# Two batches take turns in the sums of their shared chunk, and the planner's ranks are drawn anew

## The chip, the cores and the metric

The kernel runs on one core of a Trainium2 chip. The time is device microseconds (us) of one execution; lower is better. Several executions are timed and the median is told, and one more execution is profiled: it has a time of its own, and its span runs from its first instruction to its last.

## The reference

Attention with random features over 8 batches of 8 heads, 576 tokens and 64 channels, with 128 features, and behind it a bilinear feed-forward network over all 4608 tokens:

```
def phi(x):                                   # x scaled by 64 ** -0.25
    h = x @ omega.T - sum(x * x) / 2
    return exp(h - max(h)) / sqrt(128)
kv  = einsum('bhsm,bhsd->bhmd', phi(k), v)    # one 128 x 64 matrix per batch and head
z   = sum(phi(k), axis=2)
att = (phi(q) @ kv) / (phi(q) @ z + 1e-6)
x   = att, heads side by side                 # 4608 x 512
out = (((x @ w1) * (x @ w2)) @ w3) @ w_out    # 512 -> 1024 -> 1024 -> 512
```

## The kernel before

**Tiles.** The 4608 tokens are 36 chunks of 128 rows. A batch has 576 tokens, four chunks and a half, so chunk 4 belongs to batch 0 with its first 64 rows and to batch 1 with its last 64.

**Keys and values.** For each chunk TensorE projects the keys (`kpj`, L610 in float32 for the first chunks, L615 in pairs of float16 later), VectorE takes the maximum over the features (L643), ScalarE the exponential (L665), and the result is split into two float16 parts (L527 to L531, L686). The sum over the tokens of features times values, `kvp`, is made in float32 from whole features for batches 0 and 1 (L769, `kv_add`), and from the float16 parts for the six others (L822). `kv_add(b, n)` adds the share of batch `b` in its chunk `n`: for each of two groups of four heads one step of four matmuls, into the PSUM bank `kvp_b_g`. The whole chunks use all 128 rows of the array. The two shares of chunk 4 use rows 0 to 63 and rows 64 to 127; batch 0's two steps come first and close its banks, then batch 1's two steps open theirs. When the last share of a batch is in, ScalarE moves its two banks out (L782, `kv_exact`), and `kv_parts` makes float16 parts of them. The profile shows each float32 matmul as two records.

**Queries.** They go the same way, then are turned by DMA (`eqT`), multiplied by the batch's matrix (`nu`, L902 and L908), divided and turned again (`xT`).

**Weights.** They arrive as 64-bit floats, 1 MB at a time (L1054, into one of three places called `raw`), and ScalarE, VectorE and GpSimd make float32 of them in five steps (L1057, L1063, L1066, L1070, L1079). The product of `w3` and `w_out` is made in eight blocks of sixteen float32 matmuls (`wp`, L1150). `w1` and `w2` get sums of their magnitudes (`l`, L1106), a scale (`ws`, L1123) and float16 parts (L1133).

**The network.** For chunks 0 to 7 it is `gate` (`ab`, L1196), from chunk 8 on `seven_gate`, a form with seven block products in place of eight (`x` and `y`, L1303); `project_out` multiplies by the product matrix (`o`, L1530).

**The order.** No loop fixes it. Each step is an operation with an assumed duration, and the class `Plan` replays all of them: an engine that is free takes, of the operations whose inputs and buffers are there, the one with the lowest rank. The order that comes out is written into the program. A rank is a place in a hand-made timetable (`KRANK`, `QRANK`, `WRANK`, and a period of 15.1 for the later chunks) plus a correction from the table `SHIFT`, by kind and number. Loads carry `hold`: they are not begun before their rank, read as a time. Buffers of most kinds are given out in turn. Where TensorE would have nothing to do before 260 us of the replay, the plan puts in a matmul on constants, the filler (`warm`, L459). It needs a free PSUM bank of the kind `pm`, of which there are four; the sums `kvp` of batches 0 and 1, the blocks `wp`, `ab`, `x`, `y`, `o` and the small sums of squares use the same four.

Of the kernel before, what the change touches and what calls it, by code (L numbers as in the profile page):

```python
# [22 lines left out]
P = 128  # L23
# [30 lines left out]
class Plan:  # L54
# [211 lines left out]
KV_PARTS = 4.7  # L266
# [3 lines left out]
    "attend": [-261.0442, -899.7197, -80.5697, -1.7498, -497.6982, -829.27, -0.5233, 130.4034, -60.6807, -977.3105, 590.9, -139.0417, -1108.6767, -258.3056, 152.0799, -675.3894, 179.9762, -129.9433, -156.7907, -531.4993, -603.8193, 184.7717, 169.6617, -1403.3389, 90.1091, -577.3232, 242.8103, 80.48, 87.4543, -540.7832, -24.3105, 130.0178, 497.3243, -219.6722, -908.4751, -817.6591],  # L270
    "fetch": [-320.1924, -257.6749, -303.305, -248.9927, -252.9728, -161.6177, -170.7265, -141.0951, 0.0, -68.9231, 11.8978, 0.0, 18.3653, -56.175, -98.2639, -172.3054, -4.3852, 8.0229, 6.9409, 11.3851, 0.0, 9.4996, 8.3504],
    "gate": [45.0201, -55.6099, 53.21, -242.9426, 211.0326, -147.4938, -186.7604, -112.2666, 234.1896, -62.4668, 351.9161, -553.5163, -101.3645, -184.3984, 21.6502, -6.2693, 205.244, 884.0132, 0.0, 0.0, -146.1711, -55.9723, 0.0, 0.0, 105.9104, 213.7739, 0.0, 0.0, 74.0634, 182.5986, 0.0, 0.0, -59.026, 392.9282, 0.0, 0.0, -269.9867, 15.1283, 0.0, 0.0, -416.4902, -203.1226, 0.0, 0.0, -26.4861, 683.023, 0.0, 0.0, 107.705, 121.6833, 0.0, 0.0, 369.2073, 337.3498, 0.0, 0.0, 253.0506, 236.1074, 0.0, 0.0, -273.608, -60.1419, 0.0, 0.0, -120.9892, -52.692, 0.0, 0.0, 12.4493, -100.2414],
# [20 lines left out]
EXACT_B = 2  # L293
# [40 lines left out]
def tile_favor_attention_then_bilinear_ffn(  # L334
# [383 lines left out]
    def v_batch(b):  # L718
# [18 lines left out]
        for c, r0, r1 in cs:  # L737
# [3 lines left out]
            def ends(t=t, r0=r0, r1=r1):  # L741
                if r1 - r0 < P:
# [11 lines left out]
                    t.ap[r0:r1, 0, :, 0:D], ALU.mult, ALU.subtract,  # L754
                ),
                r=[x, s, (t, 0)], w=[(t, 1)], port=BOTH)

    kv_sum = [[Buf("pm", f"kvp_{b}_{g}") for g in range(2)] for b in range(EXACT_B)]

    def kv_add(b, n):  # L760
        cs = chunks_of(b)
        c, r0, r1 = cs[n]
        last = n == len(cs) - 1

        def add(g):
            t = kv_sum[b][g].ap[:, 0 : 4 * E].rearrange("p (i e) -> p i e", e=E)
# [821 lines left out]
    for c in range(NCH):  # L1588
# [26 lines left out]
        if c >= PROJECT_K and c - AHEAD >= alone:  # L1615
            plan.at("q", c - AHEAD, q_rank(c - AHEAD))
            q_chunk(c - AHEAD, c - AHEAD < FAST_Q)
# [95 lines left out]
```

## Time and profile before

| | |
|---|---|
| median of 3 timed runs | 776.56 us (773.46 to 778.33) |
| the profiled execution: its time, its span | 771.27 us, 769.5 us |
| TensorE busy | 746.3 us (97%), 10458 instructions |
| VectorE busy | 639.0 us (83%) |
| ScalarE busy | 488.7 us (64%) |
| GpSimd busy | 263.7 us (34%) |
| mean granted clock of TensorE | 0.999 |
| read from and written to HBM | 49.50 MB and 9.44 MB |

Engines are named PE (TensorE matmuls), PEld (its weight loads), DVE (VectorE), ACT (ScalarE), POOL (GpSimd) and SP (SyncE, which issues DMAs). A granted clock of 1.00 is the higher of TensorE's two levels, 2.4 GHz. Busy time counts fillers too.

### The profile page before, as it was taken

Reading aid. Unit: us, or ns where it says so; the run is one execution under the profiler, and the core shown is the slowest. Engines: PE = TensorE matmul, PEld = TensorE weight load, DVE = VectorE, ACT = ScalarE, POOL = GpSimd, SP = SyncE. Lnnn points to the kernel's source line nnn. Section 1 sums busy time; section 2 is a strip of 40 time slices with the busy share of each in tenths; the row PEclk is TensorE's granted clock in tenths of the full one; section 3 lists DMA queues with packets and bytes.
Section 4 is the critical chain, followed back from the end, with each engine's and each line's share of the span. In section 5 each row is a group of like instructions: output and inputs, shape, how many; then the busy total and the mean of one; then the engine's idle time right before and its main releaser. Section 6 shows DMA issues by size and latency. Waiting matters only on the chain.

```text
span 769.5 us, 24553 instructions
## 1 busy us (share of the span) xinstructions
PE 746.3 (97%) x10458; PEld 589.1 (77%) x10466; DVE 639.0 (83%) x1178; ACT 488.7 (64%) x952; POOL 263.7 (34%) x314
## 2 busy tenths in 40 slices
PE   8999999999999999999999999999999999999998
PEld 7756558886757787778787868789877968789784
DVE  6899899999998878979989899998798687787332
ACT  5857575787898956867776568675665455434221
POOL 2301005535621434254442275624433162511000
PEclk9999999999999999999999999999999999999999
DMA  9897852333463645555456447553543345444101
GB/s 340 308 260 219 233 152 84 112 98 72 103 145 112 143 114 86 118 85 148 105 95 146 112 112 174 104 112 78 105 98 77 84 84 116 79 97 72 42 15 42
DMA packets 166909, 93.82 MB, mean 122 GB/s; under 512 B 136976, under 2 KB 145296, under 8 KB 166800
## 3 DMA queue, kind: packets, MB, share of 16 engines
q1 hardware_dynamic: 158784, 79.60, 44.0%
q10 hardware_dynamic: 8016, 12.65, 5.2%
q8 instruction: 82, 1.34, 0.7%
q14 instruction: 27, 0.22, 0.1%
HBM read 49.50 MB, written 9.44 MB: 77 GB/s over the span
## 4 chain that ended last, share of the span: by engine, by line
PE 52%; DVE 29%; DMA 6%; ACT 5%; issue 5%; POOL 2%; SPq 0%; ACTq 0%; DVEq 0%; POOLq 0%
PE o L1530 14%; PE x L1303 13%; PE y L1303 10%; PE ab L1196 4%; PE wp L1150 3%; PE nu L908 2%; DVE nm_k L643 2%; PE qpj L615 2%; DVE arena L1070 2%; DVE nm_q L643 2%; PE kvp L822 2%; DMA arena<-wo 2%; DMA eqT<-eq 1%; DVE eq L686 1%; DVE vhl L752 1%
## 5 line engine op out<-in xcount | busy, mean ns | idle before, releaser
L1303 PEld LDWEIGHTS <-arena 128*128 128x128 f16 x2688 | 152.9, 98 | 6.1 <-issue 1.8
L1303 PEld LDWEIGHTS <-w12b 128*128 128x128 f16 x2016 | 114.3, 98 | 3.3
L1530 PE MATMUL o<-Wb,w12b 128*128 128x512 f16 x408 | 93.8, 379 | 0.0
L1196 PE MATMUL ab<-xT,w12b 128*128 128x128 f16 (+1 forms) x1152 | 88.7, 237 | 1.6 <-DVE ws L1123 1.3
L1196 PEld LDWEIGHTS <-w12b 128*128 128x128 f16 x1152 | 80.4, 98 | 10.3 <-issue 2.0
L1303 PE MATMUL x<-xT,arena 128*128 128x128 f16 x1344 | 84.2, 219 | 0.8 <-ACT u_u L1320 0.4
L1303 PE MATMUL y<-xT,arena 128*128 128x128 f16 x1344 | 84.2, 219 | 0.5 <-DVE asb_s L1326 0.5
L1303 PE MATMUL x<-xT,w12b 128*128 128x128 f16 x1344 | 82.5, 219 | 0.0
L1530 PEld LDWEIGHTS <-w12b 128*128 128x128 f16 x408 | 38.5, 98 | 42.4 <-issue 0.5
L1530 PE MATMUL o<-Wb 128*128 128x512 f16 x276 | 63.8, 379 | 0.2 <-POOL Wb L1337 0.2
L1530 PEld LDWEIGHTS <-Wb 128*128 128x128 f16 x276 | 26.0, 98 | 29.1 <-POOL Wb L1337 0.7
L643 DVE TENSOR_REDUCE nm_q<-qpj 128x8 f32<-128x1024 f32 x36 | 43.7, 1215 | 5.0 <-PE qpj L615 5.0
L643 DVE TENSOR_REDUCE nm_k<-kpj 128x8 f32<-128x1024 f32 x36 | 43.6, 1215 | 2.8 <-PE kpj L615 1.9
L1539 ACT ACTIVATE o<-o,oscs 128x512 f32<-128x512 f32 x36 | 24.8, 688 | 33.0 <-PE o L1530 30.0
L676 ACT ACTIVATE e_q<-e_q,ln_e,es_q 128x1024 f32<-128x1024 f32 x25 | 31.0, 1240 | 19.0 <-DVE e_q L672 14.1
L1530 PE MATMUL o<-Wb,arena 128*128 128x512 f16 x180 | 41.7, 379 | 0.5 <-ACT asb L1208 0.5
L1303 PE MATMUL y<-xT,w12b 128*128 128x128 f16 x672 | 42.1, 219 | 0.0
L686 DVE TENSOR_TENSOR eq<-e_q,eq 128x1024 f16<-128x1024 f32 x26 | 33.6, 1292 | 4.5 <-ACT eq L527 3.4
L1324 DVE TENSOR_TENSOR u_u<-x,u_u 128x512 f32<-128x512 f32 x28 | 19.2, 687 | 20.9 <-PE x L1303 20.4
L908 PEld LDWEIGHTS <-eqT 128*128 128x128 f16 (+1 forms) x936 | 29.4, 100 | 7.7 <-issue 3.1
L908 PE MATMUL nu<-kv,eqT 128*128 128x65 f16 (+1 forms) x936 | 32.0, 193 | 2.6 <-DMA eqT<-eq 2.3
L1000 ACT ACTIVATE xw_x<-xw_x,p2r_x 128x512 f32<-128x512 f32 x28 | 20.0, 717 | 21.7 <-DVE p2r_x L520 21.3
(238 smaller groups left out, 1633.3 us busy)
## 6 DMA issues: line engine op xcount, KB each, us to landing
vraw<-v SPq DMA_DIRECT2D x36, 260.0 KB, 3.7
qraw<-qT SPq DMA_DIRECT2D x36, 256.0 KB, 3.0
kraw<-kT SPq DMA_DIRECT2D x36, 256.0 KB, 3.2
out<-o SPq DMA_DIRECT2D x36, 256.0 KB, 2.4
arena<-w3T ACTq DMA_DIRECT2D x6, 1024.0 KB, 5.9
arena<-w ACTq DMA_DIRECT2D x6, 1024.0 KB, 5.3
arena<-wo SPq DMA_DIRECT2D x4, 1024.0 KB, 7.5
arena<-w3T SPq DMA_DIRECT2D x2, 1024.0 KB, 7.5
```

Source lines behind the costliest of these rows:

```text
L615: nc.tensor.matmul(pg[:, g, i], hls[name, c].ap[d, x, i], om[d, y], start=n == 0, stop=n == len(PASSES) - 1)
L643: one(DVE, 1.22, lambda: nc.vector.tensor_reduce(nm.ap, pj_of(pa), AX.X, ALU.max, negate=True), r=[pa], w=[nm], new=[nm])
L676: one(ACT, 1.23, lambda: nc.scalar.activation(e.ap, e.ap, AF.Exp, scale=factor(), bias=ln_e), r=key, w=[e])
L686: engine(g).tensor_tensor(f16(t.ap)[:, 1], e.ap, f16(t.ap)[:, 0], ALU.subtract)
L908: nc.tensor.matmul(n_[r0:r1, h // 4, h % 4], f16(t.ap)[:, x, place(h), r0:r1], kv_view(kvs[b])[:, y, h], start=n == 0, stop=n == 2,)
L1000: one(ACT, 0.72, lambda: nc.scalar.mul(flat(xs), flat(xs), r.ap), r=[r], w=[xs])
L1150: nc.tensor.matmul(bank.ap, w[:, j], guest[:, j], start=j == 0, stop=j == NF - 1)
L1196: nc.tensor.matmul(dst, w12[m][i][cc][:, a, r * P : (r + 1) * P], x.ap[:, b, cc, off : off + T], start=j == 0, stop=j == len(mm) - 1,)
L1303: nc.tensor.matmul(dst()[:, f * P : (f + 1) * P], ws[c][0]()[:, a, f * P : (f + 1) * P], xv(c, b), start=start and f == 0 and j == 0, stop ...
L1324: one(DVE, 0.69, lambda: nc.vector.tensor_tensor(f32(t), dst(), f32(t), ALU.add), r=[key], w=[t], rank=first)
L1530: nc.tensor.matmul(bank.ap, hs[c, f][1]()[:, a], W[f][:, b], start=f0 + i == 0, stop=f0 + 4 == NF and i == len(mm) - 1,)
L1539: one(ACT, 0.67, lambda: nc.scalar.mul(o.ap, bank.ap, sc), r=[bank, ("osc", c)], w=[o], new=[o], rank=rank - 1000)
```

## The change

`kv_add` takes a list of shares. A whole chunk has one share and is added as before. Chunk 4 has two, and they are one call now: for each group of four heads one step of eight matmuls, in which for each head batch 0's matmul on rows 0 to 63 is followed by batch 1's on rows 64 to 127, into their two banks. So the step holds a bank of each batch, and opens batch 1's while it closes batch 0's. The plan assumes 0.62 us for such a step, where it assumed 0.94 us for each of four smaller ones, and batch 1's extra delay of `KV_PARTS` is gone; the two shares have one rank, that of number 4 of the kind `kv`, and number 5 is not used. Besides, every number of `SHIFT` that was not zero is another one: all ranks of all kinds. Of the 22 kinds the diff shows three here.

```diff
-    "fetch": [-320.1924, -257.6749, -303.305, -248.9927, -252.9728, -161.6177, -170.7265, -141.0951, 0.0, -68.9231, 11.8978, 0.0, 18.3653, -56.175, -98.2639, -172.3054, -4.3852, 8.0229, 6.9409, 11.3851, 0.0, 9.4996, 8.3504],
+    "fetch": [-925.3345, -824.8687, -542.9285, -450.6918, -535.714, -378.1459, -382.3202, -197.542, 0.0, -64.6442, -36.7066, 0.0, -41.7227, -79.9913, -175.1455, -278.5055, -110.7568, -9.3466, -14.5852, -15.7422, 0.0, -0.7951, -23.1963],
...
-    "kv": [158.5124, -158.4609, -162.7804, -150.9707, -232.8124, -145.8852, -391.2947, -100.8073, 3.6608, -482.1456],
+    "kv": [-100.7299, -528.6885, -690.7509, -418.2748, 112.2776, 0.0, 423.4926, -147.2643, 569.9348, 218.7368],
...
-    "unit": [-522.9387, -317.9578, -322.7961, -303.0594, -300.9332, -217.673, -199.3355, -141.0736, -973.4887, -80.9006, 14.191, -73.1609, 23.3492, -24.603, -104.8843, -198.5929, -11.0785, 15.999, -2.7909, 29.5605, 81.4712, 34.6026, 111.1784, 182.8732, 238.4257],
+    "unit": [-1451.7847, -1375.0192, -1357.2705, -1064.5022, -1000.9318, -710.22, -563.0267, -429.5976, 266.1431, -5.4514, 14.5282, 104.5733, 38.5182, -52.7715, -121.3134, -488.4972, -94.1638, 6.3287, 168.2541, 222.0637, 349.3645, 304.6784, 412.186, -18.4507, 84.1356],
...
-    def kv_add(b, n):
-        cs = chunks_of(b)
-        c, r0, r1 = cs[n]
-        last = n == len(cs) - 1
+    def kv_add(*shares):
 
         def add(g):
-            t = kv_sum[b][g].ap[:, 0 : 4 * E].rearrange("p (i e) -> p i e", e=E)
             for i in range(4):
                 h = 4 * g + i
-                nc.tensor.matmul(
-                    t[:, i], ekf[c].ap[r0:r1, place(h)], vraw[c].ap[r0:r1, h],
-                    start=n == 0 and i == 0, stop=last and i == 3,
-                )
-
+                for b, n in shares:
+                    cs = chunks_of(b)
+                    c, r0, r1 = cs[n]
+                    t = kv_sum[b][g].ap[:, 0 : 4 * E].rearrange("p (i e) -> p i e", e=E)
+                    nc.tensor.matmul(
+                        t[:, i], ekf[c].ap[r0:r1, place(h)], vraw[c].ap[r0:r1, h],
+                        start=n == 0 and i == 0, stop=n == len(cs) - 1 and i == 3,
+                    )
+
+        c, r0, r1 = chunks_of(shares[0][0])[shares[0][1]]
         for g in range(2):
-            one(PE, 0.94, lambda g=g: add(g), r=[ekf[c], (vraw[c], 0), (vraw[c], 1)],
-                w=[kv_sum[b][g]], new=[kv_sum[b][g]] * (n == 0), mode=P if r1 - r0 == P else D)
+            banks = [kv_sum[b][g] for b, _ in shares]
+            one(PE, 0.94 if r1 - r0 == P else 0.62, lambda g=g: add(g), r=[ekf[c], (vraw[c], 0), (vraw[c], 1)],
+                w=banks, new=[kv_sum[b][g] for b, n in shares if n == 0], mode=P if r1 - r0 == P else D)
...
+        shares = [(b, n) for b in range(EXACT_B) for n, x in enumerate(chunks_of(b)) if x[0] == c]
+        if shares:
+            plan.at("kv", c + shares[0][0], r)
+            kv_add(*shares)
         for b in range(EXACT_B):
-            for n, (x, _, _) in enumerate(chunks_of(b)):
-                if x == c:
-                    plan.at("kv", c + b, r + (KV_PARTS if b and not n else 0))
-                    kv_add(b, n)
             if last_of.get(c) == b:
```

The numbers of `unit` and `fetch` follow the string `ooooWW11a22bWWWWWW11a22bS`: `o` is a quarter of `w_out`, `W` a block of the product, `1` and `2` a quarter of `w1` or `w2`, `a` and `b` the split of a half of `w1` or `w2`, `S` the split of the product.

## Rows read from the trace of the kernel before

**Rows 1.** The page, part 1, TensorE alone; part 2, its granted clock.

```profile
PE 746.3 (97%) x10458; PEld 589.1 (77%) x10466; DVE 639.0 (83%) x1178; ACT 488.7 (64%) x952; POOL 263.7 (34%) x314
...
PEclk9999999999999999999999999999999999999999
```

**Rows 2.** Busy time by stage; sixth column of engines is granted clock.

```profile
0.00:36.00 36.00, 32.84 (x314) 27.64 (x315) 28.87 (x42) 23.84 (x65) 9.51 (x34) 1.00 0.93 332
36.00:160.00 124.00, 117.74 (x1099) 82.55 (x1106) 115.21 (x197) 80.93 (x167) 29.36 (x28) 1.00 0.61 172
160.00:460.00 300.00, 291.00 (x4310) 230.60 (x4308) 266.81 (x516) 226.26 (x468) 125.41 (x142) 1.00 0.51 113
460.00:765.66 305.66, 304.71 (x4748) 248.31 (x4744) 228.16 (x425) 156.97 (x255) 99.44 (x111) 1.00 0.40 87
765.66:769.50 3.84, 0.00 (x1) 0.00 (x0) 0.00 (x0) 0.69 (x1) 0.00 (x0) 0.88 0.17 68
```

**Rows 3.** The same stages, instructions on the tile warm alone.

```profile
0.00:36.00 36.00, 9.79 (x66) 0.20 (x1) 1.00 0.93 332
36.00:160.00 124.00, 6.00 (x52) 0.00 (x0) 1.00 0.61 172
```

**Rows 4.** Waits of TensorE, 0 to 160 us: total, times, longest.

```profile
PE l L1106 <- ACT o_wab L1098: 1.7, 1, 1.7
PE wp L1150 <- DVE arena L1079: 1.5, 1, 1.5
PE ab L1196 <- DVE ws L1123: 1.3, 1, 1.3
PE wp L1150 <- DVE xT L1079: 1.3, 1, 1.3
```

**Rows 5.** The same list for 160 to 460 us.

```profile
PE norm_q L493 <- ACT junk L487: 3.4, 5, 1.2
PE nu L908 <- DMA eqT<-eq: 2.3, 2, 1.6
```

**Rows 6.** Timeline of TensorE, 0 to 60 us: start, length, what, idle before.

```profile
26.69 2.00 PE L769 MATMUL kvp<-vraw,ek_f 128*128 128x65 f32 x16
29.03 1.16 PE L610 MATMUL kpj<-o_om_raw,kraw 64*128 64x128 f32 x16 [0.34 <-ACT ek_f L665]
30.02 2.40 PE L769 MATMUL kvp<-vraw,ek_f 64*128 64x65 f32 x24
32.79 1.10 PE L769 MATMUL kvp<-vraw,ek_f 64*128 64x65 f32 x8 [0.37 <-ACT kv_f L782]
...
33.87 1.47 PE L459 MATMUL warm<-ones 128*128 128x256 bf16 x12
35.47 7.11 PE L1150 MATMUL wp<-w12b,xT 128*128 128x512 f32 x16
```

**Rows 7.** Timeline of all engines, 28 to 37 us.

```profile
31.32 1.14 ACT L1057 ACTIVATE arena<-arena 128x1024 f32<-128x1024 f32 x1 [2.35 <-DMA arena<-w3T]
...
32.35 0.66 ACT L782 ACTIVATE kv_f<-kvp 128x260 f32<-128x260 f32 x2
...
34.11 1.22 DVE L1079 SCALAR_TENSOR_TENSOR xT<-arena 128x1024 uint32<-128x1024 uint32 x1
```

**Rows 8.** Timeline of SyncE, 0 to 60 us: its DMA issues.

```profile
2.12 0.43 SPq L1054 DMA_DIRECT2D arena<-wo  x1
...
18.31 0.38 SPq L1054 DMA_DIRECT2D arena<-wo  x1
```

**Rows 9.** Busy time in the stretch 100 to 220 us.

```profile
100.00:220.00 120.00, 114.21 (x1479) 91.99 (x1483) 116.54 (x216) 91.09 (x198) 56.49 (x45) 1.00 0.40 102
```

**Rows 10.** Groups by line and shape: VectorE work of one key chunk.

```profile
L643 DVE TENSOR_REDUCE nm_k<-kpj 128x8 f32<-128x1024 f32 x36 | 43.6, 1215 | 2.8 <-PE kpj L615 1.9 <-PE kpj L610 0.7
...
L686 DVE TENSOR_TENSOR ek<-e_k,ek 128x1024 f16<-128x1024 f32 x17 | 21.6, 1270 | 1.5 <-ACT ek L527 0.9 <-POOL ek L531 0.4
...
L590 DVE SCALAR_TENSOR_TENSOR hlk_k<-kraw,s_q,hlk_k 128x512 f16<-128x512 f32 x25 | 20.6, 823 | 0.0
```

More of the change, by code (lines that the diff above doesn't have):

```diff
@@ L272 @@
-    "gate": [45.0201, -55.6099, 53.21, -242.9426, 211.0326, -147.4938, -186.7604, -112.2666, 234.1896, -62.4668, 351.9161, -553.5163, -101.3645, -184.3984, 21.6502, -6.2693, 205.244, 884.0132, 0.0, 0.0, -146.1711, -55.9723, 0.0, 0.0, 105.9104, 213.7739, 0.0, 0.0, 74.0634, 182.5986, 0.0, 0.0, -59.026, 392.9282, 0.0, 0.0, -269.9867, 15.1283, 0.0, 0.0, -416.4902, -203.1226, 0.0, 0.0, -26.4861, 683.023, 0.0, 0.0, 107.705, 121.6833, 0.0, 0.0, 369.2073, 337.3498, 0.0, 0.0, 253.0506, 236.1074, 0.0, 0.0, -273.608, -60.1419, 0.0, 0.0, -120.9892, -52.692, 0.0, 0.0, 12.4493, -100.2414],
[9 rows of a table removed]
@@ L282 @@
-    "out": [-376.514, 497.2412, 63.8815, -68.9294, -790.7933, 891.007, -0.2063, 162.7468, -307.3469, 677.8557, 275.8913, 105.9823, 300.0604, -563.3277, 370.8116, 1120.3123, -636.2116, 38.8286, -5.1696, 269.1214, 780.3382, 886.5999, 899.8989, -746.3036, 532.6139, 601.5237, -365.0474, -87.4787, 222.8698, -417.0185, -590.3117, -61.4904, -1288.133, 152.0269, 215.2352, -197.548],
-    "pair": [0.0, 0.0, 0.0, 0.0, 0.0, 0.0, 0.0, 0.0, 0.0, 0.0, 0.0, -69.1469, -420.1598, -350.3318, -1467.0095, 13.5062, -1262.8946, 161.0739, 3.1468, -107.8226, -868.2686, -207.1637, -4.9551, -125.6928, 59.6855, -846.6351, 70.1117, -179.4445, 39.5746, -99.3894, -178.0142, 666.0484, -383.5356, 215.1784, 582.7228, 3.0289],
[5 rows of a table removed]
@@ L289 @@
-    "sum": [11.8372, 1491.9104, -128.3876, 359.8411],
-    "unit": [-522.9387, -317.9578, -322.7961, -303.0594, -300.9332, -217.673, -199.3355, -141.0736, -973.4887, -80.9006, 14.191, -73.1609, 23.3492, -24.603, -104.8843, -198.5929, -11.0785, 15.999, -2.7909, 29.5605, 81.4712, 34.6026, 111.1784, 182.8732, 238.4257],
-    "v": [0.0, 0.0, 289.4843, -41.9162, 317.7933, 338.429, 193.7706, 295.9627],
+    "attend": [-33.9644, -588.7958, -245.2466, 112.6694, 51.3394, 623.7508, -211.7652, -49.8193, 1.1812, -586.9079, 1809.2974, -184.659, -2377.44, -259.9265, -49.4813, -2.2019, -105.5111, 198.3123, 28.0357, -56.1994, -123.9714, 5.3923, -19.9446, 86.3289, 70.3568, 186.7349, 77.7578, 454.5261, -23.0736, -693.9705, -159.068, -511.3347, -748.5079, -72.6846, 331.0986, 368.0839],
@@ new lines @@
+    "fetch": [-925.3345, -824.8687, -542.9285, -450.6918, -535.714, -378.1459, -382.3202, -197.542, 0.0, -64.6442, -36.7066, 0.0, -41.7227, -79.9913, -175.1455, -278.5055, -110.7568, -9.3466, -14.5852, -15.7422, 0.0, -0.7951, -23.1963],
+    "gate": [481.8676, 164.6381, 249.9083, 992.1741, 1575.3487, -332.7836, -306.4834, -286.4339, -368.3007, -330.7792, 89.3306, -106.6537, -152.6991, 63.7717, 469.0214, 553.3953, -28.276, 962.2678, 0.0, 0.0, -1724.903, -89.3212, 0.0, 0.0, -941.0957, -54.4385, 0.0, 0.0, -46.177, -47.5723, 0.0, 0.0, -184.5281, 130.4981, 0.0, 0.0, 161.2236, 270.4674, 0.0, 0.0, 409.8437, 393.5028, 0.0, 0.0, 133.38, 619.7029, 0.0, 0.0, 278.6571, 446.1498, 0.0, 0.0, 657.3535, -170.8092, 0.0, 0.0, -59.2993, 25.8461, 0.0, 0.0, 297.6619, 266.9017, 0.0, 0.0, -605.7172, 238.8639, 0.0, 0.0, 203.6933, 325.2007],
[9 rows of a table added]
@@ new lines @@
+    "out": [400.6419, 663.3448, 676.3232, 88.4737, 76.7119, 1035.9881, 1201.8732, 591.8491, -1466.2665, 351.619, -510.5236, 436.3716, 847.5083, 709.8632, 93.8906, 30.7097, -588.3518, 486.9493, 722.7325, -262.5307, 1540.2584, -47.0963, 641.4933, -854.8927, -421.9015, 1090.9892, 37.749, -55.6569, 103.9235, 946.5714, -411.2674, -596.0518, 264.3718, 519.464, 581.4619, -211.4359],
+    "pair": [0.0, 0.0, 0.0, 0.0, 0.0, 0.0, 0.0, 0.0, 0.0, 0.0, 0.0, 3.662, -395.4164, -451.9309, -838.4994, 137.6582, 145.8825, 204.8484, -596.2423, -131.866, -141.167, -1014.6718, -266.9878, -243.0172, -175.477, 108.9952, -1395.2751, -201.6946, 210.5917, -557.766, 542.4946, -153.7914, 345.9352, 1.6867, 114.7156, 198.7281],
[5 rows of a table added]
@@ L292 @@
+    "sum": [475.2533, 1275.59, 364.1564, 272.3384],
+    "unit": [-1451.7847, -1375.0192, -1357.2705, -1064.5022, -1000.9318, -710.22, -563.0267, -429.5976, 266.1431, -5.4514, 14.5282, 104.5733, 38.5182, -52.7715, -121.3134, -488.4972, -94.1638, 6.3287, 168.2541, 222.0637, 349.3645, 304.6784, 412.186, -18.4507, 84.1356],
+    "v": [0.0, 0.0, 89.2966, -6.4304, 95.271, 636.1417, -831.1163, 57.8691],
 }
```

1 line of the change is left out of this document (removed), and 26 rows, old and new, of the table SHIFT.

## The prediction

> **What bounds the kernel now.** I read the page first: TensorE is busy 97% of the span at the upper of its two clock levels from the first slice to the last [rows 1], so neither the clock nor a slow stage explains anything, and what is left is time in which TensorE waits or does nothing useful. Then the stages [rows 2]. TensorE lacks 3.2 us of the first 36, 6.3 us of the stage from 36 to 160, 9.0 us of that from 160 to 460, and 1.0 us of the 305.7 after that; the last 3.8 us are the final eviction and its store, which no order removes. Busy time also holds fillers, which compute nothing: 9.8 us in the first stage and 6.0 us in the second, none later [rows 3]. Idle time and fillers together, without the tail, are therefore 12.9, 12.3, 9.0 and 1.0 us, 35 us in all: 4.6% of the span is the most that any order could give. Third, what ends the waits. From 36 to 160 us four single waits hold 5.8 of the 6.3 us, and behind each is a weight on its way: two product blocks for the last conversion step (1.5 and 1.3 us), a magnitude sum for ScalarE (1.7 us), a gate for its scale (1.3 us) [rows 4]. Later they are small and scattered, first the norms behind ScalarE's squares, 3.4 us in five pieces [rows 5].
>
> VectorE is the second limit. From 100 to 220 us it works 116.5 of 120 us [rows 9], so in that stretch a step that it owes to TensorE is as late as the others put before it.
>
> Beside these rows, a rule of the Trainium skill, "Perfetto Trace Analysis", section "Identifying the Most-Contended Engine": matmul occupancy says little of the distance to the roofline, and weight-load occupancy is to be used. By that the room would be the 23% that PEld lacks [rows 1]. It would be room for other matmuls, not for another order: from 460 us on TensorE is all but gapless while PEld has 248 of 306 us [rows 2]. I keep the 35 us as ceiling.
>
> **The chunk of two batches.** Now it takes three steps in one run, 24 records in 2.40 us, then 0.37 us of waiting, then 8 records in 1.10 us [rows 6]: 3.50 us of work and 0.37 us idle. In each step all matmuls lie on one half of the rows, 100 ns a record in the long run. After the change the halves alternate. The nearest row is the exact projection, also float32 and alternating between the halves: 16 records in 1.16 us, 73 ns each, with 128 columns where the sums have 65 [rows 6]. That is the dear end, 32 x 73 = 2.32 us; the cheap end is half of the 100 ns, 1.60 us. So 1.2 to 1.9 us of TensorE time go. I take 1.5 us, from the middle, since the row has twice the columns and so is a ceiling.
>
> The wait is less sure. The new steps open batch 1's bank while batch 0's is open, so the pair of steps needs four of the four banks, unless the first evicted one is waited for. Before, the last step waited for the same thing: ScalarE was in a weight conversion of 1.14 us and then did two evictions in 0.66 us [rows 7]. Now the wait can be nothing (0.37 us gained) or one conversion and one eviction, 1.14 + 0.33 = 1.47 us (1.1 us lost). The Trainium skill says as much of the cause, in "TensorEngine Tiling (Array Packing)", section "Gotcha 1: PSUM Pressure": row tiles must write to different banks, so packing costs banks. The 0.37 us fits that. By the rule alone the second step always waits.
>
> Work and wait together lie between 2.3 us gained and 0.1 us gained. Little of it is on the path. Behind the sums stands 1.47 us of filler, and the first product block begins at 35.47, when VectorE's last conversion step, 34.11 + 1.22 = 35.33, is through [rows 6, 7]. Shorter sums make more filler. I enter **0**, with 2.3 us of gain if something else is ready to fill the place, and 1.5 us of loss if the longer wait also holds batch 0's eviction and the cover is gone.
>
> **The ranks.** No row of the trace shows an order that has not run, so I bound it. What the diff lets one work out by hand are the loads' ranks, since a fetch is held until timetable - 12 + its correction. The last three blocks of the product that the plan holds, numbers 12, 16 and 17, go from 44, 50 and 69 to -16, -57 and 52 us; the last quarter of `w2` goes from 98 to 67. All six late product blocks are fetched at an earlier rank. Nothing of them is on the other side of the ledger at once: the loads of the first queries that were let in at 13 or 15 (4 and 1) go to -59 and 27, and SyncE issues the first 1 MB fetch at 2.12 us and the fourth only at 18.31, when a `raw` place is free [rows 8]; that place, not the rank, sets the early rate, and I enter 0 for the first stage (bounds: 1 us either way, about what moving one 0.26 MB load past a 1 MB fetch is worth at 332 GB/s [rows 2]: 0.8 us). For the second stage I credit the earlier fetches with the two waits of product blocks, 1.3 + 1.5 = **2.8 us** [rows 4]. The splits of `w1` and `w2` get later ranks (three of four: -917 to 322, -9 to 169, 175 to 443), while their fetches get earlier; the two waits for them, 1.7 + 1.3 us, I leave as they are. Bounds: all 12.3 us of that stage's idle time and fillers gained, or the loss that the second rival prices. From 160 to 460 us no rank says more than that the order is another; the waits there are small, and I enter 0, between half of their 9.0 us gained and as much lost. Later VectorE has slack and TensorE is full: 0.
>
> **The sum.** 0 + 0 + 2.8 + 0 = 2.8 us. The profiled execution took 771.27 us for a span of 769.5, so 1.8 us lie outside; it becomes 768.5. The median of the runs is 5.3 us above it, and the runs shown lie between 773.46 and 778.33; I carry the same 2.8 us over: 776.56 - 2.8 = **773.8 us**. About 1%, 7.8 us here, is what a measurement of this kernel tells from no change: faster means below 768.8, slower above 784.3.
>
> **Rivals.** *The stage of the weights closes up.* Earlier fetches end the weight stream earlier, and the fillers behind the last magnitude sums go as well. For it: the waits there all end with a weight. Against it: `raw` places come free only when a conversion is done, and VectorE does those among its other work. All 12.3 us: 776.6 - 12.3 = 764.3.
>
> *The splits starve.* With rank 322 the first split of `w1` stands on VectorE's list behind every key and query step that is ready; gates need it. One key chunk puts 1.215 + 1.270 + 0.823 = 3.31 us in front of it [rows 10]; three chunks are 9.9 us, in which TensorE has no gate to run and shows fillers: 776.6 + 9.9 = 786.5. It decides from the second chunk on (6.6 us eat the gain and more). For it: VectorE has only 3.5 us free of 120 [rows 9]. Against it: before 100 us VectorE has more slack, the split is made of small steps, and buffers of key chunks are few, so that the list is often short.
>
> *The change doesn't pair.* If the matmuls of the two halves run one after the other, the sums stay at 3.50 us and the wait at up to 1.47 us. At most 1.1 us worse, hidden as above: 773.8 to 774.9.
>
> **How the numbers follow.** The forecast, with the pairless case in it, has 0.55 (own range 768.8 to 778.8: 5 us on either side for half of the middle stage's waits and the bounds of the first); the closing stage, and anything else above 1%, 0.25; starving splits, and other orders that lose over 1%, 0.20. The range 764 to 785 takes in the first rival and reaches to just short of the second's 786.5; 2 in 10 are left out.
>
> **What would show it.** In the timeline of TensorE the chunk's sums should be 32 records of 64 rows in 1.6 to 2.3 us, in one or two pieces, with filler or another step behind them and the first product block no earlier than its conversion. The waits of product blocks between 36 and 160 us should be below 1 us, while fillers stay between 10 and 20 us. Starving splits would show as a first gate over 10 us later than now and over 10 us of fillers in that stage; a closed stage as under 5 us of idle time and filler there. The prediction is wrong if the middle stage moves by more than its 9.0 us, if TensorE shows idle time past 460 us, or if VectorE's order leaves it idle between 100 and 220 us.

## The result and the profile after

| | before | changed |
|---|---|---|
| median of 18 runs each | 775.99 us (772.74 to 781.16) | 770.17 us (764.05 to 780.66) |
| the profiled execution: its time, its span | 771.27 us, 769.5 us | 766.23 us, 764.4 us |

The ratio is 0.9907 with a 95% interval from 0.9879 to 0.9935: 7.2 us faster, clear of noise, and just under the 1% that was called faster. (The ratio leaves disturbed runs out, so it does not follow from the two medians.) The changed kernel spreads more: its runs lie within 17 us, those of the kernel before within 8.

The page of the changed kernel, part 1 and the granted clock of part 2; compare [rows 1]:

```profile
PE 743.4 (97%) x10423; PEld 585.3 (77%) x10423; DVE 625.6 (82%) x1163; ACT 490.0 (64%) x953; POOL 287.8 (38%) x328
...
PEclk9999999999999999999999999999999999999999
```

TensorE's busy time fell by 2.9 us, the span by 5.1. VectorE has 13.4 us less to do than before and GpSimd 24.1 us more, since the new order gives some steps that either can do to GpSimd. Busy time by stage, with the columns of [rows 2] (the busy time of PE, PEld, DVE, ACT, POOL, then granted clock, DMA share, GB/s):

```profile
0.00:36.00 36.00, 31.93 (x314) 27.02 (x316) 26.53 (x36) 20.89 (x54) 7.32 (x32) 1.00 0.86 299
36.00:160.00 124.00, 118.69 (x1087) 82.16 (x1084) 116.91 (x201) 85.11 (x177) 31.08 (x27) 0.99 0.63 174
160.00:460.00 300.00, 293.86 (x4480) 234.91 (x4478) 269.34 (x526) 234.83 (x487) 144.15 (x170) 0.99 0.56 122
460.00:760.60 300.60, 298.86 (x4552) 241.25 (x4549) 212.84 (x404) 148.52 (x237) 105.25 (x101) 1.00 0.42 82
```

and the fillers in the same stages, as in [rows 3]:

```profile
0.00:36.00 36.00, 10.62 (x75) 0.20 (x1) 1.00 0.86 299
36.00:160.00 124.00, 0.00 (x0) 0.00 (x0) 0.99 0.63 174
```

Idle time and fillers together:

| stage, us | before | changed |
|---|---|---|
| 0 to 36 | 3.2 + 9.8 = 13.0 | 4.1 + 10.6 = 14.7 |
| 36 to 160 | 6.3 + 6.0 = 12.3 | 5.3 + 0 = 5.3 |
| 160 to 460 | 9.0 | 6.1 |
| from 460, without the tail | 1.0 | 1.7 |

The middle stage gave 7.0 us, the next 2.9; the first and the last took 2.5 back. Before rounding that is 7.3 us, but the span fell by 5.1: TensorE's busy time without fillers grew by 2.2 us, from 746.3 - 15.8 = 730.5 to 743.4 - 10.6 = 732.7 us, although the sums of chunk 4 got shorter. The granted clock of 0.99 in two stages says why, and the experiments follow it up: each of these two stages holds 1.7 us by which work got longer, so up to that much of its gain may be slower work in the place of idle time.

What ends TensorE's waits up to 160 us, for [rows 4]; then the first of the list from 160 to 460 us, for [rows 5]:

```profile
PE kvp L769 <- POOL vraw L716: 2.2, 1, 2.2
PE wp L1152 <- ACT Wb L1157: 2.2, 2, 1.8
PE ab L1198 <- DVE asb L1212: 1.3, 1, 1.3
...
PE ab L1198 <- DVE ws L1125: 0.9, 1, 0.9
...
PE l L1108 <- ACT o_wab L1100: 0.3, 1, 0.3
```

```profile
PE norm_q L493 <- ACT junk L487: 2.0, 1, 2.0
```

The wait for a magnitude sum fell from 1.7 to 0.3 us. Product blocks still wait 2.2 us, for another engine: ScalarE, which has to move the block before them out. And the fillers of the middle stage are gone. The kernel before has them from 139 to 145 us, ahead of the gate behind the last scale, and has the whole-chunk sums of three chunks of batch 1 between 72 and 87 us (its timeline of TensorE; the first row is one of the three sums):

```profile
72.35 2.00 PE L769 MATMUL kvp<-vraw,ek_f 128*128 128x65 f32 x16
...
139.03 3.33 PE L459 MATMUL warm<-ones 128*128 128x256 bf16 x29
...
147.46 2.24 PE L1196 MATMUL ab<-xT,w12b 128*128 128x128 f16 x37 [1.29 <-DVE ws L1123]
```

The changed kernel has these sums later, one ahead of the last product block and two behind the first gate at 111.3 us, so that gates are left for the place of the fillers. The last row is again the gate behind the last scale:

```profile
95.81 1.98 PE L769 MATMUL kvp<-vraw,ek_f 128*128 128x65 f32 x16
...
115.06 1.98 PE L769 MATMUL kvp<-vraw,ek_f 128*128 128x65 f32 x16
...
117.31 1.89 PE L769 MATMUL kvp<-vraw,ek_f 128*128 128x65 f32 x16
...
144.57 10.28 PE L1198 MATMUL ab<-xT,w12b 128*128 128x128 f16 x181 [0.89 <-DVE ws L1125]
```

### The profile page after: what moved, and what is told of

It reads as the page before. It is cut to its first block, busy times and chain, and to the rows that moved or that the text cites. A ratio compares the mean times of both kernels' runs of the same rounds, so it can differ in the third digit from the quotient of the medians.

```text
span 764.4 us, 24509 instructions
## 1 busy us (share of the span) xinstructions
PE 743.4 (97%) x10423; PEld 585.3 (77%) x10423; DVE 625.6 (82%) x1163; ACT 490.0 (64%) x953; POOL 287.8 (38%) x328
## 4 chain that ended last, share of the span: by engine, by line
PE 57%; DVE 23%; DMA 8%; ACT 6%; issue 4%; POOL 2%; SPq 0%; ACTq 0%; DVEq 0%; POOLq 0%
PE o L1532 18%; PE x L1305 15%; PE y L1305 11%; PE ab L1198 5%; PE nu L910 2%; PE qpj L615 2%; DVE arena L1072 2%; DMA arena<-wo 2%; PE kvp L824 2%; DMA vraw<-v 2%; PE kpj L615 1%; DVE w12b L1135 1%; DVE nm_q L643 1%; PE wp L1152 1%; ACT vhl L471 1%
## 5 line engine op out<-in xcount | busy, mean ns | idle before, releaser
L1305 PEld LDWEIGHTS <-arena 128*128 128x128 f16 x2688 | 152.3, 98 | 4.9 <-issue 1.0
L1532 PE MATMUL o<-Wb,w12b 128*128 128x512 f16 x396 | 91.2, 379 | 0.3 <-DVE u_u L1328 0.3
L1532 PE MATMUL o<-Wb,arena 128*128 128x512 f16 x204 | 46.5, 379 | 0.0
L686 POOL TENSOR_TENSOR eq<-e_q,eq 128x1024 f16<-128x1024 f32 x15 | 32.2, 2144 | 16.5 <-ACT eq L527 14.9
L1532 PEld LDWEIGHTS <-arena 128*128 128x128 f16 x204 | 19.4, 98 | 21.8
L1059 ACT ACTIVATE arena<-arena 128x1024 f32<-128x1024 f32 x20 | 23.4, 1174 | 18.7 <-DMA arena<-w 6.4
L665 ACT ACTIVATE e_k<-kpj,nm_k,es_q 128x128 f32<-128x128 f32 x88 | 32.0, 487 | 5.0 <-DVE nm_k L656 4.5
```

What stands on the lines that cost most here:

```text
L665: nc.scalar.activation(e.ap[:, h], pj()[:, h], AF.Exp, scale=factor(), bias=nm.ap[:, h : h + 1])
L686: engine(g).tensor_tensor(f16(t.ap)[:, 1], e.ap, f16(t.ap)[:, 0], ALU.subtract)
L1059: one(ACT, 1.14, lambda: nc.scalar.activation(mag.ap, words(1).bitcast(F32), AF.Abs), r=[raw], w=[mag], new=[mag])
L1305: nc.tensor.matmul(dst()[:, f * P : (f + 1) * P], ws[c][0]()[:, a, f * P : (f + 1) * P], xv(c, b), start=start and f == 0 and j == 0, stop ...
L1532: nc.tensor.matmul(bank.ap, hs[c, f][1]()[:, a], W[f][:, b], start=f0 + i == 0, stop=f0 + 4 == NF and i == len(mm) - 1,)
```

## Experiments

Each ratio is to the kernel before, run on the same chip at the same time. Two chips were used. On the first (pairing undone, all experiments with ranks, the moved write, the moved load, both with fillers) the kernel before has medians of 773.5 and 773.9 us; on the second (work left out, fillers, both moves without fillers) 776.2. Ratios that are 0.3% apart and come from different chips need not mean a difference.

### The pairing undone

```diff
-            for i in range(4):
-                h = 4 * g + i
-                for b, n in shares:
+            for b, n in shares:
+                for i in range(4):
+                    h = 4 * g + i
```

> The changed kernel with one thing undone: in each of the two steps of chunk 4 batch 0's four matmuls come first and batch 1's four behind them, so the row halves do not alternate; the order of all engines' other work stays as it is. Pairing does what it says: the 32 half-row records take 3.2 to 3.5 us in place of about 1.9, the first product block starts 1 to 1.5 us later, and the time is 0 to 1.5 us above that of the changed kernel (ratio to the kernel before 0.990 to 0.993). Pairing does nothing: the 32 records take 1.9 us here too. Pairing is the whole gain: the ratio goes back to 0.998 or more.

Ratio 0.9888 (0.9834 to 0.9942), median 765.96 us. The groups by shape around chunk 4, the changed kernel (from 30 to 37 us) and this one (from 33 to 40 us): records, busy us, mean ns.

```profile
L769 PE MATMUL kvp<-vraw,ek_f 64*128 64x65 f32 x32 | 2.0, 275 | 0.0
```

```profile
L769 PE MATMUL kvp<-vraw,ek_f 64*128 64x65 f32 x32 | 2.6, 278 | 0.0
```

The timelines, changed kernel first. In each the first row holds the 16 records of chunk 3 as well; the second fence ends with the first product block:

```profile
31.65 3.93 PE L769 MATMUL kvp<-vraw,ek_f 128*128 128x65 f32 x48
35.41 1.11 PE L610 MATMUL qpj<-o_om_raw,qraw 64*128 64x128 f32 x16
36.46 7.13 PE L1152 MATMUL wp<-w12b,xT 128*128 128x512 f32 x16
```

```profile
33.20 4.20 PE L769 MATMUL kvp<-vraw,ek_f 128*128 128x65 f32 x45
...
38.62 7.13 PE L1152 MATMUL wp<-w12b,xT 128*128 128x512 f32 x16
```

The changed kernel takes 2.0 us for the 32 half-row records, some 62 ns each. Without turns they take 2.6 us, 81 ns each. The long piece alone, with chunk 3, takes 4.20 us for 45 records against 3.93 for 48, and the last three records stand one by one between those of the next projection. From the start of chunk 3's sum to the product block it is 5.42 us in place of 4.81. So taking turns is worth 0.6 us on this path, less than the 1 to 1.5 us that were expected: 3.2 to 3.5 us were expected for the 32 records without turns, but runs of 8 on one half, in place of the 16 of the kernel before, already cost 81 ns a record in place of 100. In the time it is not to be seen. The whole gain is there without it.

### New sums, old ranks

All of `SHIFT` as in the kernel before, and

```diff
-            one(PE, 0.94 if r1 - r0 == P else 0.62, lambda g=g: add(g),
+            one(PE, 0.94 if r1 - r0 == P else 1.5, lambda g=g: add(g),
```

> The new code of the sums with all ranks of the kernel before; the plan assumes 1.5 us for a step of chunk 4, by which its order of the first 150 us stays close to that of before. The gain is the new ranks': the stage from 36 to 160 us keeps idle time and fillers of 9 to 15 us and the ratio is 0.995 to 1.01. The gain is the pairing's: the ratio is 0.993 or less, and that stage loses under 8 us.

Ratio 1.0574 (1.0525 to 1.0624), median 819.5 us: neither. The middle stage has 3.0 us idle and 6.8 of fillers, as the first case had it, but from 160 to 460 us there are 15.8 us idle and 19.8 of fillers. The ranks of before belong to the order of before; the same ranks with one step merged give another order, and a bad one, in which the gain or loss by the new sums can't be read.

### Batch 1's keys moved by themselves

The changed kernel with the old ranks of chunks 5 to 8 in the kinds `k`, `load k`, `load v`, of numbers 6 to 9 of `kv` and of number 1 of `kv parts`:

```diff
-    "kv": [-100.7299, -528.6885, -690.7509, -418.2748, 112.2776, 0.0, 423.4926, -147.2643, 569.9348, 218.7368],
+    "kv": [-100.7299, -528.6885, -690.7509, -418.2748, 112.2776, 0.0, -391.2947, -100.8073, 3.6608, -482.1456],
...
-    "kv parts": [-1147.2677, -123.1805],
+    "kv parts": [-1147.2677, -0.2658],
```

> The changed kernel with the old ranks of that group alone (loads, key features and sums of chunks 5 to 8), which puts all of these sums before the last product blocks, as in the kernel before. Late keys fill the hole: idle time and fillers from 36 to 160 us rise from 5.3 to 10 us or more, and the ratio to the kernel before is 0.995 to 1.01. Earlier weight fetches are the cause: the stage stays at 4 to 7 us and the ratio at 0.988 to 0.994.

Ratio 1.0518 (1.0467 to 1.0569), median 815.87 us. Busy time in the second and third stage, then the fillers there:

```profile
36.00:160.00 124.00, 121.01 (x1084) 84.08 (x1081) 110.08 (x188) 79.51 (x166) 30.93 (x27) 1.00 0.60 170
160.00:460.00 300.00, 276.72 (x4065) 225.92 (x4063) 250.61 (x494) 217.10 (x455) 135.12 (x150) 0.96 0.50 108
```

```profile
36.00:160.00 124.00, 7.75 (x68) 0.00 (x0) 1.00 0.60 170
160.00:460.00 300.00, 18.72 (x164) 0.00 (x0) 0.96 0.50 108
```

The middle stage loses 3.0 + 7.8 = 10.8 us, twice what the changed kernel loses there: that part of the forecast for late keys holds. The total says nothing about it, since the third stage loses 23.3 + 18.7 = 42 us in an order that nobody sought.

The reverse, the kernel before with the new ranks of the same steps:

```diff
-    "kv": [158.5124, -158.4609, -162.7804, -150.9707, -232.8124, -145.8852, -391.2947, -100.8073, 3.6608, -482.1456],
+    "kv": [158.5124, -158.4609, -162.7804, -150.9707, -232.8124, -145.8852, 423.4926, -147.2643, 569.9348, 218.7368],
...
-    "kv parts": [-332.0836, -0.2658],
+    "kv parts": [-332.0836, -123.1805],
```

> The kernel before with the new ranks of one group of steps alone: the key and value loads, key features and sums of chunks 5 to 8 (batch 1), which puts three of these sums behind the first gates, where the changed kernel has them. Late keys fill the hole: no filler between 130 and 150 us, idle time and fillers from 36 to 160 us fall from 12.3 to 8 us or less, ratio 0.990 to 0.997 unless later stages lose. The earlier weight fetches are the cause: the stage keeps 10 us or more. Neither can be parted from the rest of the ranks: the stage changes by less than 3 us and the total by more, with the sign open.

Ratio 1.0735 (1.0677 to 1.0793), median 830.84 us. The middle stage loses 7.6 + 1.9 = 9.5 us in place of 12.3: fillers fall from 6.0 to 1.9 us, but waits rise. The later stages lose 46.5 and 16.5 us. Of the three cases that were expected this is the third: the stage changed by 2.8 us, the total by far more, and the two causes are not parted.

Idle time and fillers of the middle stage, taken together: 12.3 us with the old ranks, 10.8 with all new ranks but those of these keys, 9.5 with the new ranks of these keys alone, 5.3 with all. The 10.8 are with the new ranks of the weight fetches, so earlier fetches alone don't close the stage; late keys alone don't either. All four orders differ in other places too, so this is a hint and not a proof.

Ranks could not be parted any further in this way, so the next experiments keep an order as it is and leave work out of it.

### Work left out of a fixed order

The changed kernel without the matmuls of chunks 6 to 8 in the sums of batch 1 (those sums are left out of the result):

```diff
                 for b, n in shares:
+                    if b == 1 and n > 1:
+                        continue
...
-                        start=n == 0 and i == 0, stop=n == len(cs) - 1 and i == 3,
+                        start=n == 0 and i == 0, stop=n == (1 if b else 4) and i == 3,
```

> The changed kernel, same order, without the matmuls of the sums of chunks 6, 7 and 8 of batch 1 (six steps, 5.8 us of TensorE between 93 and 119 us); that part of the result is left out. If the stage up to 145 us is bound by the weights' conversion and these steps only fill its holes, the last scale is waited for until 143 to 145 us as before, and the time falls by less than 2 us, or not at all. If TensorE is the bound there, the step behind the last scale begins 5 to 6 us earlier and the time falls by 5 to 6 us.

Ratio 0.9875 (0.9827 to 0.9923), median 767.96 us: 0.3% under the changed kernel, with intervals that overlap. TensorE's middle stage, and two waits in its timeline:

```profile
36.00:160.00 124.00, 106.85 (x903) 69.87 (x903) 109.41 (x188) 79.86 (x167) 28.10 (x24) 0.94 0.64 165
```

```profile
102.24 1.48 PE L912 MATMUL nu<-kv,eqT 128*128 128x65 f16 x24 [8.76 <-ACT ek_f L665]
...
151.91 8.27 PE L1200 MATMUL ab<-xT,w12b 128*128 128x128 f16 x145 [0.88 <-DVE ws L1127]
```

5.8 us of work are gone and 17.2 us are idle where 5.3 were. The gate behind the last scale came at 151.9 us, not earlier. So TensorE's work is not the bound there, and the sums lie largely in holes. How far is not to be read from this execution: the first row shows something that the changed kernel's profile has only in small: `nu` waited 8.76 us for ScalarE, 0.41 there, and the granted clock stood at 0.50 for some 13 us from 98 us on. It comes back below.

The kernel before without the same steps:

```diff
                 h = 4 * g + i
+                if b == 1 and n > 1:
+                    continue
...
```

> The kernel before, same order, without the same six steps (between 72 and 87 us there). Bound by the weights: the wait for the last scale still ends at 146 to 148 us, fillers and idle time take the place of the steps, and the time falls by less than 2 us. Bound by TensorE: it ends 5 to 6 us earlier.

Ratio 0.9969 (0.9946 to 0.9992), median 774.74 us: 2.4 us of 5.8, against the forecast of under 2 for the weights' bound and of 5 to 6 for TensorE's, so neither as it was put. Two rows of its timeline:

```profile
78.98 9.85 PE L1152 MATMUL wp<-w12b,xT 128*128 128x512 f32 x16 [3.86 <-DVE xT L1081]
...
150.12 2.24 PE L1198 MATMUL ab<-xT,w12b 128*128 128x128 f16 x37 [1.29 <-DVE ws L1125]
```

The last scale came 2.7 us later than in the kernel before. Without the sums a product block waited 3.86 us for its conversion, and then took 9.85 us in place of 7.1, at a granted clock of 0.50 from about 78 to 84 us.

The changed kernel with one VectorE step of the conversion left out for `w1` and `w2`:

```diff
-            lambda: nc.vector.tensor_scalar(
+            lambda: name[:2] in ("w1", "w2") or nc.vector.tensor_scalar(
                 g(), g(), 3, 0x3FFFFFFF, ALU.logical_shift_left, ALU.bitwise_and
             ), w=[mag], port=BOTH)
```

> The changed kernel, same order, with one VectorE step of the conversion (0.69 us each) left out for the eight quarters of w1 and w2, 5.5 us of VectorE in all, so that their values are wrong. If the conversions on VectorE set the end of the stage, the wait for the last scale ends 3 to 6 us earlier than 144.6 us and the time falls by 2 to 5 us. If the places of the fetches or their transfers set it, or TensorE does, it ends within 1.5 us of where it was and the time falls by less than 1.5 us.

Ratio 0.986 (0.981 to 0.991), median 766.87 us: 0.5% below the changed kernel's ratio, with intervals that overlap.

```profile
99.74 1.48 PE L910 MATMUL nu<-kv,eqT 128*128 128x65 f16 x24 [5.28 <-ACT ek_f L665]
...
147.50 10.28 PE L1198 MATMUL ab<-xT,w12b 128*128 128x128 f16 x181 [0.20 <-DVE ws L1125]
```

The wait for the last scale fell to 0.20 us. The point itself, 147.5, is later than the 144.57 of the changed kernel, since this execution had the long wait of `nu` too. Counted from `nu`, the gate stood 49.5 us behind it in the changed kernel, 49.7 in the one without late sums, and here 47.8. That looks like 1.8 us of the 5.5 us that VectorE was spared, but the kernel with the pairing undone, which has the changed kernel's order here and all of its work, shows the same:

```profile
96.11 0.90 PE L910 MATMUL nu<-kv,eqT 128*128 128x65 f16 x24
...
144.04 10.28 PE L1198 MATMUL ab<-xT,w12b 128*128 128x128 f16 x181 [1.16 <-DVE ws L1125]
```

It is 47.9 us from `nu` to the gate there, at a granted clock of 1.00, while in the three others the last product block or the steps ahead of it ran in part at 0.50. So what sets the end of the stage, VectorE's conversions, the arrival of the weights or both, stays open.

### The clock behind TensorE's waits

The changed kernel's profile has two places where the granted clock halves. TensorE in windows of 1 us (busy, clock, DMA share, GB/s), then the steps that stand there:

```profile
99.00:100.00 1.00, 0.00 (x0) 1.00 1.06 115
...
102.00:103.00 1.00, 1.00 (x2) 0.50 0.95 334
...
337.00:338.00 1.00, 0.00 (x0) 1.00 0.19 33
...
341.00:342.00 1.00, 1.00 (x3) 0.50 0.23 48
```

```profile
100.53 8.83 PE L1152 MATMUL wp<-w12b,arena 128*128 128x512 f32 x16 [1.85 <-ACT Wb L1157]
```

```profile
338.94 0.16 PE L493 MATMUL norm_q<-sums_q,ones 128*128 128x2 bf16 x1 [2.03 <-ACT junk L487]
...
340.33 4.40 PE L1532 MATMUL o<-Wb 128*128 128x512 f16 x12
```

The product block took 8.83 us where its neighbours take 7.1, and the run of `o` 4.40 us where it takes 2.75: 1.7 us each, 3.4 in all. Less the 1.5 us that the sums gave, that leaves 1.9 of the 2.2 us by which useful busy time grew. A rule of the Trainium skill, "TensorE: Matmul & The Clock Gate", section "What's actually happening", is that the gate knows the half and the full clock, and falls when the engine has been idle. The trace agrees, with 0.50 and 1.00 and idle time ahead of both falls, though not every such wait is followed by a fall (the last section has two that were not). The times of all runs go the same way: the changed kernel's 18 runs have a mean granted clock from 1.000 (764.5 us) to 0.982 (780.66 us). An estimate: if the stretches at 0.50 had taken half as long, a run's time times its mean clock would be left. That lies between 761.0 and 767.1 us for the 18 runs, so the clock goes with most of their spread. For the runs of the kernel before that stand beside the experiments it lies between 770.2 and 775.9 us.

Fillers in front of six steps that wait, in the order as it was, into a PSUM bank that the plan has free there:

```diff
+FILL = {305: (14, False), 148: (14, False), 1793: (6, False), 500: (6, False), 728: (14, True), 1094: (8, False)}
...
+            if o.part and o.no in FILL:
+                n, own = FILL[o.no]
+                f = copy(o.new[0]) if own else Buf(self.spare[o.no][0][0], "fill")
...
+                for _ in range(n):
+                    self.filler.ways[PE][1](f)
             fn()
```

> The changed kernel, same order on all engines, with 62 fillers (0.11 us each) put in front of six TensorE steps that wait in its profile (the third key chunk's sum, the last product block, a gate behind the last scale, two norms, one projection), so that TensorE runs on constants while it waits. If the falls of the granted clock to 0.50 behind the waits at 100.5 and 338.9 us come of those waits, both are gone from the profile, the granted clock is 0.997 or more in most runs, the median falls to 763 to 767 us and the spread of the runs halves: ratio 0.982 to 0.988. If the clock falls for another reason, it is spread over the runs as before (0.982 to 1.0), and the fillers cost 0 to 2 us: ratio 0.990 to 0.994.

Ratio 0.9827 (0.9789 to 0.9865), median 765.18 us: an interval just below that of the changed kernel. By the medians of all runs it is 0.986 against 0.9925. So fillers that help are likely, but not shown; the two ratios come from different runs of the kernel before, and below the same fillers bring nothing beside the moves. The spread of the runs, 17 us, did not halve. Five of its eight runs have a granted clock of 0.999 or 1.000, and they lie between 761.85 and 765.7 us; of the changed kernel's 18 runs one has. Three runs, 769.05, 773.59 and 778.82 us, do not fit. The second of them is the profiled one, and its timeline of TensorE names the place:

```profile
100.23 1.48 PE L927 MATMUL nu<-kv,eqT 128*128 128x65 f16 x24 [5.92 <-ACT ek_f L682]
```

Here `nu` waited 5.92 us, and the clock stood at 0.50 from 100 to 108 us. Following that wait back, GpSimd and ScalarE of this execution:

```profile
97.57 0.11 POOL L733 MEMSET vraw<- 128x8 f32 x1 [22.99 <-DMA vraw<-v]
97.77 0.20 POOL L673 TENSOR_SCALAR nm_k<-nm_k 128x8 f32<-128x8 f32 x1
```

```profile
98.00 2.18 ACT L682 ACTIVATE ek_f<-kpj,nm_k 128x128 f32<-128x128 f32 x8 [4.57 <-POOL nm_k L673]
```

and GpSimd and TensorE of the changed kernel's profile at the same place:

```profile
92.43 0.11 POOL L716 MEMSET vraw<- 128x8 f32 x1 [17.01 <-DMA vraw<-v]
92.63 0.20 POOL L656 TENSOR_SCALAR nm_k<-nm_k 128x8 f32<-128x8 f32 x1
```

```profile
95.08 0.90 PE L910 MATMUL nu<-kv,eqT 128*128 128x65 f16 x24 [0.41 <-ACT ek_f L665]
```

GpSimd writes the column of ones of value chunk 8, and may do so only when that chunk has landed. Behind it in GpSimd's queue stands the bias of key chunk 6 (0.20 us of work), behind that ScalarE's exponentials, and behind those the two banks that `nu` needs. The load was issued among 1 MB fetches, at 85.1 us in the changed kernel's profile and at 85.8 in the other, and was there 7.2 and 11.6 us later, at 92.3 and 97.4 us. The Trainium skill has the rule for the queue, in "PSUM — Partial Sum Buffer", section "Engine vs sequencer instructions": the queues of ScalarE, VectorE and GpSimd are strictly first in, first out. These rows agree: the bias, 0.20 us of work, starts right behind the write of the ones in both, at 92.63 and 97.77 us.

### The late value chunk

In the fixed order of the changed kernel, the write of the ones moved behind the bias and two weight steps, or the load moved ahead of two other loads:

```diff
+        done = self.order()
+        for no, behind in ((362, 161),):
+            x = next(d for d in done if getattr(d[3], "no", None) == no)
+            done.remove(x)
+            done.insert(next(i for i, d in enumerate(done) if getattr(d[3], "no", None) == behind) + 1, x)
...
```

(for the load, the pair is 361 and 1332.)

> The changed kernel, same order but for one step: GpSimd's write of the ones column of value chunk 8, which waits for that chunk's load, stands behind the bias of key chunk 6 and a weight step in place of ahead of them. If the wait of nu at 95 to 100 us (0.4 us in one profile, 5.3 to 8.8 us in others) comes of this step at the head of GpSimd's queue, it is 1 us or less in the profile, runs over 772 us become rare, and the ratio is 0.982 to 0.988. If the wait comes of something else that is late there (the weights' transfers themselves), it stays at 0.4 to 9 us from run to run and the ratio at 0.988 to 0.994.

> The changed kernel, same order but for one step: SyncE issues the load of value chunk 8 about 20 us earlier, ahead of the loads of the fifth query and the seventh key chunk, so that it does not travel among two 1 MB fetches. If the late landing of this load is what GpSimd waits for, the wait of nu is 1 us or less and the ratio 0.982 to 0.988, as with the write moved. If it is not, ratio 0.988 to 0.994.

The write moved: ratio 0.9875 (0.9828 to 0.9922), median 763.14 us of five. The load moved: 0.9884 (0.9838 to 0.9929), median 764.07 us of five. Both profiles have a span of 759.1 and 759.6 us, a granted clock of 1.000, and no wait of `nu` at that place. GpSimd with the write moved, and TensorE's gate behind the last scale:

```profile
87.91 0.20 POOL L661 TENSOR_SCALAR nm_k<-nm_k 128x8 f32<-128x8 f32 x1 [13.86 <-DVE nm_k L648]
...
97.34 0.11 POOL L721 MEMSET vraw<- 128x8 f32 x1
```

```profile
140.13 10.28 PE L1203 MATMUL ab<-xT,w12b 128*128 128x128 f16 x181 [1.15 <-DVE ws L1130]
```

The bias runs 4.7 us earlier, and the last scale is there at 140.1 us, 4.4 earlier than in the changed kernel's profile. With the pairing undone, on the same chip and without a move, the bias came at 92.81 us and the gate at 144.04. So the step at the head of GpSimd's queue is what holds the bias. That it makes the long wait of `nu` is likely: the three profiles of the unmoved order on the second chip have waits of 5.3 to 8.8 us there, and the one with both moves on that chip (below) has none. These two profiles alone don't say so, since with the pairing undone `nu` didn't wait either. That it makes the time is not shown: the medians are 6 to 7 us below the changed kernel's, but the kernel before was 2.5 us faster beside them too, and the ratios' intervals overlap with the changed kernel's. The ratio of the moved write lies in the range that was expected if this is the cause, that of the moved load just outside it.

Both moves with the fillers:

> Both moves together with the 62 fillers in front of the six waiting steps. If late loads behind GpSimd's queue and the clock's falls behind TensorE's waits are the two things that spread the runs of the changed kernel, the runs lie within 760 to 768 us with a granted clock of 0.997 or more in nearly all, and the ratio is 0.978 to 0.985. If one of the two is not a cause, the ratio is that of the fillers alone, 0.983, or above.

Ratio 0.9887 (0.9844 to 0.9929), median 765.15 us of six. Four runs have a clock of 1.000 and lie between 762.26 and 765.32 us; two lie at 770 and 771.6 us. The ratio is not that of the two causes together, 0.978 to 0.985, and no better than with the pairing undone, 0.9888, which has neither move nor filler. The profiled execution, 769.99 us, still has a wait of `nu` of 1.75 us, behind a 1 MB fetch for which ScalarE waited 4.32 us, and a clock of 0.50 both behind that wait and from 16 to 20 us, behind a wait of 1.66 us that none of the fillers is put at. So other late transfers and other places remain. The fillers' own cost shows: at a clock of 1.000 the kernels with a move and no fillers ran in 760.9 to 761.7 us.

Both moves without fillers:

> The changed kernel with both moves (the load of value chunk 8 earlier, the write of its ones later) and no fillers. If each move takes the same wait away and nothing else, the two together are like either alone: median 761 to 765 us, ratio 0.982 to 0.988, the wait of nu at 95 us 1 us or less. If a second late transfer takes its place, the runs still spread to 770 us and more with a granted clock under 0.993, and the ratio is 0.988 to 0.992.

Ratio 0.9867 (0.9837 to 0.9898), median 765.62 us of six; three runs with a clock of 0.993 or 0.994. The wait of `nu` is gone from the profile, which is of a run at 1.000; what lowers the clock in the others is not seen. Of the versions that leave nothing out, the fillers alone have the best ratio, and the fastest single runs are those without fillers (760.57 us with the pairing undone, 760.9 with the write moved); which is best in the long run is not settled.

## Why the prediction was right, and where it was not

The time came out 3.6 us below the forecast, inside the range, and inside the band that had the most weight. That is in part luck: the one term that was entered came by another way and more than twice as large, and the clock, which was in no term, took back 3.4 us of it in the profiled execution. Point by point:

- **The sums of chunk 4.** Forecast 1.6 to 2.3 us for the 32 records, measured 2.0, so 1.5 us less than the 3.50 of [rows 6], as taken there. Only 0.6 of the 1.5 us are the turns inside a step; the rest remains with the pairing undone. The wait between the steps did not come, so the reading by which the second step always waits was wrong. Entered as 0 on the path; undoing it left the ratio at 0.9888. Right.
- **The first stage.** Entered as 0 with 1 us either way; it lost 1.7 us more, and holds a new wait of 2.2 us for a value chunk's ones, the same kind of step that later holds up `nu`. Bound too narrow.
- **The middle stage.** This is the term that went wrong, in its way and in its size: 2.8 us were credited to the two waits of product blocks, 7.0 were gained, and by another way. Product blocks still wait 2.2 us, where the text wanted under 1. The fillers of this stage went, which the prediction kept, and the sums of batch 1 had moved later, two of three chunks behind the first gate. That they fill holes is borne out by leaving them out (no earlier end) and by moving them back (10.8 us lost there), in orders and executions that differ in more than that. The late ranks of the `kv` sums were in the diff and were not read for this. Earlier fetches have a share that no run parts from it: the last product block begins at 100.53 us in place of 104.27, and the last 1 MB fetch is issued at 110.5 us in place of 115.0. The rival of the closed stage had the place: it priced 12.3 us, of which 7.0 came, and 5.3 us of idle time were left where it put under 5.
- **The splits of `w1` and `w2`.** Entered as unchanged; the waits for the last sum and scale fell from 3.0 to 1.2 us, and another of 1.3 us for VectorE came. No starving: the first gate stood at 111.3 us in both kernels.
- **160 to 460 us.** Entered as 0 with 4.5 either way; it gained 2.9 us, 1.2 of them if the stretched run of `o` is taken off. Right.
- **What was not in the sum.** TensorE's clock. The text named it as explaining nothing, which was true of the profiled execution of the kernel before and not of the one after: 3.4 us in the profiled execution, and more in most others. At a clock of 1.000 the kernel before ran in 771.5 to 775.9 us and the changed one, in its one such run, in 764.5.
- **The spread carried over.** The 5.3 us between the profiled execution and the median before were carried along unchanged; after, the median lies 3.9 us above the profiled run.
- **What would have shown it wrong.** None of its three signs came clearly. The middle stage moved by 7.0 us, less than 9.0; past 460 us TensorE idles 1.7 us without the tail, 0.7 more than before; from 100 to 220 us it idles 5.4 us in place of 5.8.

The rival without a gain by the pairing is refuted by the trace. Why the new ranks are better past 160 us, if they are (the 2.9 us from 160 to 460 less the stretched run and the 0.7 us lost later leave about 0.5), is open: no part of them could be tried by itself, since every partial set cost 5 to 7%. What the work that went from VectorE to GpSimd is worth was not tried.

## What to carry to other kernels

Ranks found by a search belong to the one list of steps they were found for: changing a single step, or taking part of another set, cost 42 to 57 us against the kernel before, some thirty times the 1.5 us that the changed step was worth. Work that nothing waits for yet is best put where the engine would idle for another chain; here late sums went with the end of the fillers. And a small load issued late, with a step in an in-order queue behind it, can hold up three engines by an amount that changes from execution to execution, so a wait of 0.4 us in one profile may be 6 us in the next. When two variants differ by less than the spread that the clock makes, compare each run's time beside its granted clock, and take the chip into account.

## What the hardware showed that was not expected

- Waits of TensorE of 1.85 and 2.03 us were followed by a granted clock of 0.50 for some 3 us, at a price of 1.7 us each; a wait of 2.22 us at 27 us in the same execution was not, nor was one of 1.73 us at 134 us in the kernel before.
- 62 fillers, worth about 7 us of TensorE's busy time if nothing had waited, went with a ratio of 0.9827 in place of 0.9907, and with a clock of 0.999 or 1.000 in five of eight runs. Beside the two moves the same fillers brought no gain (0.9887 with them, 0.9867 without, on two chips).
- The landing of one 0.26 MB load among 1 MB fetches, at the same place of the order, came 6.4 us after its issue with the pairing undone, 7.2 in the changed kernel, and 11.6, 12.1 and 13.9 us with the fillers, the short conversion and the sums left out. The three long ones are all from the second chip, so whether the chip or chance makes it is not told.
